# A chunked-attention and MLP kernel on one core: the scores of two heads as a pair of half-row matmuls

## The chip, the core and the metric

The kernel runs on one core of a Trainium2 chip. TensorE multiplies matrices into PSUM, VectorE (DVE), ScalarE (ACT) and GpSimd (POOL) work on SBUF and, but for POOL, on PSUM. DMAs are issued from POOL's queue (loads from DRAM, with a cast from fp32 to fp16) and from SyncE's queue, SP (stores, copies within SBUF, and DMA transposes). The metric is the device time of one execution in microseconds; the kernel before has 217.53 us, the median of five runs from 216.94 to 217.99.

## What is computed

First comes attention in chunks, for 4 batches, 8 heads, 768 tokens and 64 dimensions a head. Each chunk of 32 queries sees 8 memory keys and the keys from 16 tokens before the chunk to 8 tokens after it. Then comes an MLP with a normed input and a residual:

```python
for c in range(S // 32):                      # per batch and head
    k_full = concat([mem_k, k[max(0, 32*c - 16) : min(S, 32*c + 40)]])
    v_full = concat([mem_v, v[the same rows]])
    a = softmax(q_c @ k_full.T / 8)
    out[chunk c] = a @ v_full
x = out as (B, S, 512)                        # heads side by side
xn = (x - mean(x)) / sqrt(var(x) + 1e-6) * g_ln
y = x + relu(xn @ w_ch1) @ w_ch2              # 512 -> 2048 -> 512
```

## The kernel before, in words

**Tiles and units.** The 3072 tokens are 24 tiles of 128, six to a batch. A tile is two groups of 64 queries (two chunks each), so a batch has NG = 12 groups. A group with its neighbours is 88 keys and 8 memory keys, held with gaps in 104 rows (KR). Eight units of three tiles make up the main loop. For each unit TensorE runs 16 up-steps (`up`, L377: one of 16 blocks of the hidden layer for 384 tokens, 4 matmuls) and 12 down-steps (`down`, L394: 4 matmuls of 512 columns). Between the steps a hand-written plan (`at(step, fn, ...)`) puts the attention of the following unit's three tiles, so each engine's order is the order in which the program writes. `attend` takes for each tile the steps of its `scores`, `values`, `norm` and `turn_x`; `root` follows three steps behind `turn_x`.

**Attention of a tile.** `scores` (L289) does 8 matmuls, one for each group and head pair: the stationary operand is a pair's keys, 128 rows (two heads of 64 dimensions), and the moving one is `QZ`, 128 columns: the 64 queries of the first head with zeros in the rows of the second, then the reverse. Then ScalarE does two exps (L296). `values` (L309) does 16 matmuls, each to one half of the output rows, and a column of ones in V gives the sums. `norm` (L319 to L329) is VectorE's. `turn_x` transposes xn, on TensorE with ScalarE's copy (L352, L357) or by a DMA.

**Keys and queries.** For batches 0 and 1 they are loaded in rows of 512 and transposed on TensorE (`turn_kq`, L179); VectorE copies keys to `KT` (`keep_k`, L194), and `keep_q` (L204) copies queries to `QZ`, 64 rows at a time, on ScalarE or VectorE. For batches 2 and 3 `load_tokens` fetches tokens and DMA transposes cross them (`cross_k` to KT, `cross_q` to `QT`, which is `kraw[1]`); POOL spreads QT into QZ (`spread_q`, L277). QZ's other halves are cleared once (`clear_q`, L436). `memv16` holds the memory values with ones; `v_mem` (L136) copies them to V by a DMA on SP.

**PSUM.** There are two `att` slots of two banks, for scores, values and transposes, and four `mm` slots of one bank. An up-step's slot is freed by the relu behind it, on VectorE for even blocks (L385) and ScalarE for odd ones (L383), and is wanted again four steps on.

**The front.** Before the loop a written order handles batch 0's first 6 groups from the first 64 rows of k (48 of q), loaded in two halves of four heads each. POOL's queue is in order k, q (heads 0 to 3), k, q (heads 4 to 7), masks and identity, six V groups, band masks, w1, and the rest. TensorE transposes with `stay_busy` (L366) fillers between, does the g_ln row (L539), the scores of tiles 0 and 1, the values of 0, the scores of 2, the values of 1 and 2, and in between up blocks on tile 0 alone, then on those that have followed. Unit 0 then begins at up-step 8, with `clear_q` for the second buffer at steps 7 and 9.

Of the kernel before, what the change touches and what calls it, by code (L numbers as in the profile page):

```python
# [8 lines left out]
FP32 = mybir.dt.float32  # L9
# [6 lines left out]
def kernel(  # L16
# [29 lines left out]
    memv16 = sb.tile([72, B, H, HD], FP16, name="memv16")[64:72, :, :, :]  # L46
    memv32 = sb.tile([72, 512], FP32, name="memv32")[64:72, :]
# [13 lines left out]
    QT = kraw[1]  # L61
# [4 lines left out]
    QZ = [sb.tile([128, NG, 4, 2, 64], FP16, name=f"QZ{i}") for i in range(2)]  # L66
    AT = [sb.tile([128, 2, H, 64], FP16, name=f"AT{i}") for i in range(3)]
# [73 lines left out]

    def load_w1(c):
        nc.gpsimd.dma_start(
            out=w1c[c], in_=dram(moe_w_ch1, 512 * c, [[FF, 128], [128 * FF, 4], [1, 512]])
        )
# [54 lines left out]
    def keep_q(copy, pv, b, j, par, n, g0, g1):  # L200


        rows = slice(64 * par, 64 * par + 64)
        copy(  # L204
            out=free(QZ[b % 2][rows, g0, j, par, :], 0, [[512, g1 - g0], [8, 8], [1, 8]]),
            in_=free(pv[rows, :], 8 * g0, [[8, g1 - g0], [1, 8], [n, 8]]),
        )

    def kq_block(b, j, g0, g1, kind, last=nc.scalar.copy):

        pk, pq = slot("att"), None
        if kind == "att":
            pq = slot("att")
            pq = [pq[:, i, :] for i in range(2)]
        else:
            pq = [slot("mm")[:, :] for i in range(2)]
        for i in range(2):
            turn_kq(as16(pk[:, i, :]), k16[b % 2], j + i, 96)
        for i in range(2):
            turn_kq(as16(pq[i]), q16[b % 2], j + i, 96)  # L220

        def keep(i):
            keep_k(as16(pk[:, i, :]), b, j + i, 96, g0 + 1 if g0 else 0, g1)
            for par in range(2):
                keep_q(last if i else nc.scalar.copy, as16(pq[i]), b, j + i, par, 96, g0, g1)

        keep(0)
        kept_later.append(lambda: keep(1))
# [11 lines left out]
    def load_tokens(b, which, t):  # L240
        dst, src = ((kraw[0], k), (qraw[0], q))[which]
        nc.gpsimd.dma_start(  # L242
            out=free(dst, 512 * t, [[64, H], [1, 64]]),
            in_=dram(src, b * H * HS + 128 * t * D, [[D, 128], [HS, H], [1, 64]]),
        )

    def cross_k(b, half, t0, t1):
        nc.sync.dma_start_transpose(
            out=free(KT[b % 2], (24 * half + 4 * t0) * KW + 16, [[KW, 4 * (t1 - t0)], [1, 64]]),
            in_=kraw[0][64 * half : 64 * half + 64, 512 * t0 : 512 * t1],  # L250
        )

    def cross_q(half, t0, t1):
        nc.sync.dma_start_transpose(
            out=free(QT, (24 * half + 4 * t0) * 64, [[64, 4 * (t1 - t0)], [1, 64]]),
            in_=qraw[0][64 * half : 64 * half + 64, 512 * t0 : 512 * t1],
        )
# [15 lines left out]
    def spread_q(b, half, t0, t1):  # L273

        for par in range(2):
            rows = slice(64 * par, 64 * par + 64)
            nc.gpsimd.tensor_copy(  # L277
                out=QZ[b % 2][rows, 6 * half + t0 : 6 * half + t1, :, par, :],
                in_=QT[rows, (24 * half + 4 * t0) * 64 : (24 * half + 4 * t1) * 64].rearrange(
                    "p (t j x) -> p t j x", j=4, x=64),  # L280
            )

    def scores(b, t):
        p = slot("att")
        a = AT[t % 3]
        for gg in range(2):
            g = place(b, 2 * t + gg)
            for j in range(4):
                nc.tensor.matmul(  # L289
                    out=p[:, gg, 128 * j : 128 * j + 128],  # L290
                    lhsT=KT[b % 2][:, (4 * g + j) * KW : (4 * g + j) * KW + 128],
                    rhs=QZ[b % 2][:, g, j, :, :],
                    start=True, stop=True,
                )
        for c in range(2):
            nc.scalar.activation(  # L296
                out=free(a, 32 * c, [[512, 2], [64, 8], [1, 32]], KR),
                in_=free(p, 32 * c, [[512, 2], [64, 8], [1, 32]], KR),
                func=ACTF.Exp, bias=band[0:KR, c : c + 1], scale=0.125,
            )  # L300
# [3 lines left out]
    def values(b, t):  # L304
        p = summed[t] = slot("att")
        for h in range(H):
            for gg in range(2):
                c0 = 128 * (h % 4)
                nc.tensor.matmul(  # L309
                    out=p[64 * gg : 64 * gg + 64, h // 4, c0 : c0 + 65],  # L310
                    lhsT=AT[t % 3][0:KR, gg, h, :],
                    rhs=V[b % 2][0:KR, 2 * t + gg, h, 0:65],
                    start=(h % 4 == 0), stop=(h % 4 == 3), tile_position=(0, 64 * gg),
                )
# [119 lines left out]
    def clear_q(i, par):  # L434

        nc.vector.memset(QZ[i][64 - 64 * par : 128 - 64 * par, :, :, par, :], 0.0)  # L436

    def clear_v(i, eng, between=lambda: None):

        eng.memset(V[i][0:32, 0, :, 0:64], 0.0)  # L440
        eng.memset(V[i][64:96, NG - 1, :, 0:64], 0.0)
        eng.memset(V[i][:, :, :, 64:HD], 1.0)
        between()
        for c, g in enumerate((0, NG - 1)):
            eng.tensor_copy(
                out=free(V[i][:, g, 0, 64:65], 0, [[HD, H]]),
                in_=free(counts[:, c : c + 1], 0, [[0, H]]),
            )
# [14 lines left out]
    nc.vector.memset(memv16[:, :, :, 64:HD], 1.0)  # L463
# [3 lines left out]
    for h in (0, 4):  # L467
        for which in range(2):
            load_kq(0, which, 0, CUT[which], h, h + 4)
    keep(counts[:, 0:1], counts[:, 0:1], 16, 0.0)  # L470
    keep(counts[:, 1:2], counts[:, 1:2], -80, 0.0)
    make_identity(nc, identity)
    nc.scalar.copy(out=memk16, in_=memk32)
    nc.scalar.copy(out=memv16[:, 0, :, 0:64], in_=memv32.rearrange("p (h d) -> p h d", h=H))
    stay_busy(10)
    clear_v(0, nc.vector, lambda: clear_q(0, 0))
    clear_q(0, 1)
    clear_k(0)
    mem_keys()
    mem_cols(0)  # L480
    stay_busy(4)
    v_mem(0)
    for g in range(6):
        load_v_group(0, g)
# [10 lines left out]
    nc.gpsimd.tensor_tensor(out=band[:, 1:2], in0=band[:, 1:2], in1=zero3[:, 2:3], op=ALU.add)  # L495
    for c in range(4):
        load_w1(c)
# [21 lines left out]
    for j in range(2):  # L519
        turn_kq(first_k[j], k16[0], j, CUT[0])  # L520
    for j in range(2):
        turn_kq(first_q[j], q16[0], j, CUT[1])
    for j in range(2):
        keep_k(first_k[j], 0, j, CUT[0], 0, 7)
        for par in range(2):
            keep_q(act, first_q[j], 0, j, par, CUT[1], 0, 6)
# [3 lines left out]
    for j in range(2, 4):  # L530
        keep_k(first_k[j], 0, j, CUT[0], 0, 7, act if j == 2 else vec)
# [3 lines left out]
    for g0, g1 in ((0, 2), (2, 6)):  # L535
        for j in range(2, 4):
            for par in range(2):
                keep_q(act if j == 2 else vec, first_q[j], 0, j, par, CUT[1], g0, g1)
    nc.tensor.matmul(out=banks[2], lhsT=ones32, rhs=g_one, start=True, stop=True)  # L539
    nc.vector.tensor_copy(out=g_row, in_=banks[2])  # L540
    scores(0, 0)
    scores(0, 1)
    stay_busy(3)
# [3 lines left out]
    scores(0, 2)  # L547
    values(0, 1)
    norm(1, 1)
    stay_busy(1)  # L550
# [3 lines left out]
    norm(2, 2)  # L554

    for hc in range(3):
        up(0, 1, hc, 0, True)
    turn_x(0, 1, 1)
    up(0, 1, 3, 0, True)
    stay_busy(2)  # L560
    for hc in range(4):
        up(0, 2, hc, 1, True)
    turn_x(0, 2, 2)
    for hc in range(4, 8):
        up(0, 2, hc)
    for hc in range(8):
        up(0, 3, hc, 2)
# [3 lines left out]
    for u, tiles in enumerate(units):  # L571
# [17 lines left out]
        def cross(steps, b, t0, t1, t2):  # L589

            for half in range(2):
                at(steps[half], cross_k, b, half, t0, t1)
                at(steps[2 + half], cross_q, half, t2 - 3, t2)

        def spread(step, b, t0, t1):
            for half in range(2):
                at(step + half, spread_q, b, half, t0, t1)

        if u == 0:
            at(7, clear_q, 1, 0)  # L600
            at(9, clear_q, 1, 1)
            at(10, clear_k, 1)
            at(23, clear_v, 1, nc.gpsimd)
            for j in (0, 2):
                at(15, kq_block, 0, j, 6, NG, "mm", nc.vector.tensor_copy if j else nc.scalar.copy)
                at(15, keep_rest)
# [7 lines left out]
            attend(((17, 19, 19, 22), (18, 21, 21, 24), (20, 23, 23, 26)), "att")  # L614
            at(26, mem_cols, 1)
            at(26, v_mem, 1)
        elif u == 1:
# [8 lines left out]
            attend(((16, 19, 19, 22), (17, 19, 20, 23), (21, 23, 23, 26)), "att")  # L626
        elif following:
            if u in (2, 4):
                attend(((2, 7, 7, 7), (4, 7, 8, 8), (9, 13, 13, 13)))
            else:  # L630
                attend(((9, 14, 14, 14), (11, 14, 15, 15), (16, 20, 20, 20)))
            if u == 2:
# [5 lines left out]
                spread(9, 2, 0, 3)  # L638
                cross((14, 14, 15, 15), 2, 4, 6, 6)
            elif u == 3:  # L640
# [3 lines left out]
                spread(5, 2, 3, 6)  # L644
# [3 lines left out]
            elif u == 4:  # L648
# [7 lines left out]
                spread(23, 3, 0, 3)  # L656
                cross((20, 21, 24, 25), 3, 4, 6, 6)
            elif u == 5:
                at(2, k_around, 3, 4, 6)
                spread(3, 3, 3, 6)  # L660
# [44 lines left out]
```

The softmax here doesn't subtract the row's maximum and nothing guards it: scores larger than these inputs give would overflow.

## Time and profile before

| what | value |
|---|---|
| median of 5 runs | 217.53 us (216.94 to 217.99) |
| the profiled execution's own time | 217.59 us |
| its span on the core | 215.9 us |
| granted TensorE clock | 0.999 |
| scores, L289, TensorE busy | 14.6 us, 192 matmuls |
| values, L309, TensorE busy | 9.5 us, 384 matmuls |
| up, L377 | 89.0 us, 560 matmuls |
| down, L394 | 84.4 us, 368 matmuls |
| exps, L296, ScalarE | 30.3 us, 48 of mean 684 ns |
| spreads of queries, L277, POOL | 13.9 us, 16 of mean 870 ns |
| clears of QZ, L436, VectorE | 5.4 us, 4 of mean 1338 ns |
| memory values by DMA, L136 | 120 KB each |

A profile is one execution. Busy times of TensorE overlap, as a matmul is counted until its result is out while the next has begun, so a matmul's price is read from the chain of work that ended last: its pieces stand in order of time with start and length. A group's line gives the code line, the engine, the operation, out<-in, the count, then busy time and the mean of one, and then the idle time before it with what ended it. PEld is the loading of TensorE's stationary operand, which overlaps PE.

### The profile page before, as it was taken

What the parts mean: (1) busy time and instruction counts of PE and PEld (TensorE: products, weight loads), DVE (VectorE), ACT (ScalarE), POOL (GpSimd) and SP (SyncE); (2) the same over time, 40 slices, a digit from 0 to 9 for tenths busy, and PEclk for the clock granted to TensorE, in tenths of its full rate; (3) what the DMA queues carried; (4) which work ended last, traced back from release to release, by engine and by line L of the source; (5) the groups of instructions that cost most, each with busy time, mean ns of one, the idle gap of its engine ahead of it and who ended that gap; (6) DMA issues with size and microseconds to landing.
All of it is one profiled execution on the core that took longest, in us unless ns stands there. A gap on an engine that the chain in (4) does not pass through costs nothing.

```text
span 215.9 us, 5059 instructions
## 1 busy us (share of the span) xinstructions
PE 209.3 (97%) x2011; PEld 129.6 (60%) x2011; DVE 118.6 (55%) x274; ACT 99.9 (46%) x206; POOL 105.1 (49%) x185
## 2 busy tenths in 40 slices
PE   7899989999999999999999999999999999999992
PEld 2557866557765577446754676457744675466562
DVE  6977774695737639514476359234484437634222
ACT  4478437865893677202753168003761275213100
POOL 7993236799996309974005998425182000300000
PEclk9999999999999999999999999999999999999999
DMA  5999999999999799996313999997643101320012
GB/s 78 180 158 206 209 207 182 199 206 227 150 139 179 89 149 143 151 148 162 45 27 89 144 185 143 149 178 110 162 125 126 49 3 24 98 101 0 0 58 91
DMA packets 87714, 27.37 MB, mean 127 GB/s; under 512 B 78297, under 2 KB 84185, under 8 KB 87642
## 3 DMA queue, kind: packets, MB, share of 16 engines
q0 software_dynamic: 62128, 14.38, 77.3%
q1 hardware_dynamic: 25562, 12.66, 27.7%
q8 instruction: 16, 0.26, 0.5%
q14 instruction: 8, 0.07, 0.1%
HBM read 28.84 MB, written 6.29 MB: 163 GB/s over the span
## 4 chain that ended last, share of the span: by engine, by line
PE 90%; DVE 3%; DMA 3%; ACT 1%; issue 1%; POOL 1%; ACTq 0%; POOLq 0%
PE mm L377 37%; PE mm L394 37%; PE att L289 5%; PE att L309 3%; DMA kraw<-in_k_dram 3%; PE att L179 2%; PE mm L412 2%; DVE QZ L436 1%; PE mm L179 1%; ACT AT L296 1%; PE att L352 1%; DVE rT L385 1%; PE mm L366 1%; PE mm L539 0%; PE att L366 0%
## 5 line engine op out<-in xcount | busy, mean ns | idle before, releaser
L377 PE MATMUL mm<-xT,w1c 128*128 128x384 f16 (+2 forms) x560 | 89.0, 313 | 0.6 <-DVE rT L385 0.5
L394 PE MATMUL mm<-w2c,rT 128*128 128x512 f16 x368 | 84.4, 379 | 0.0
L377 PEld LDWEIGHTS <-w1c 128*128 128x128 f16 x560 | 58.8, 114 | 23.6 <-issue 1.0
L383 ACT ACTIVATE rT<-mm 128x384 f16<-128x384 f32 (+2 forms) x74 | 33.2, 454 | 72.3 <-PE mm L377 50.1
L394 PEld LDWEIGHTS <-rT 128*128 128x128 f16 x368 | 34.7, 98 | 37.5
L385 DVE TENSOR_SCALAR rT<-mm 128x384 f16<-128x384 f32 (+2 forms) x66 | 35.0, 533 | 33.6 <-PE mm L377 33.5
L401 DVE SCALAR_TENSOR_TENSOR osb<-mm,rstd,xs 128x512 f32<-128x512 f32 x23 | 17.3, 751 | 41.8 <-PE mm L394 30.0
L296 ACT ACTIVATE AT<-att,band 104x512 f16<-104x512 f32 x48 | 30.3, 684 | 9.6 <-PE att L289 8.2
L338 POOL TENSOR_SCALAR veps<-squares 128x1 f32<-128x1 f32 x24 | 4.6, 191 | 44.2 <-ACT junk L335 42.9
L117 POOL DMA_DIRECT2D V<-in_v_dram x24 | 18.4, 776 | 10.3 <-DMA w1c<-in_moe_w_ch_dram 7.3
L335 ACT ACTIVATE junk<-xs,nmean 128x512 f16<-128x512 f32 x24 | 17.3, 721 | 7.1 <-DVE nmean L326 6.6
L329 DVE SCALAR_TENSOR_TENSOR xn<-xs,nmean,g_row 128x512 f16<-128x512 f32 x24 | 18.8, 783 | 0.9
L320 DVE SCALAR_TENSOR_TENSOR xs<-att,rec 128x512 f32<-128x512 f32 x24 | 16.6, 691 | 0.8
L277 POOL COPY QZ<-kraw 64x768 f16<-64x768 f16 x16 | 13.9, 870 | 4.0 <-DMA kraw<-qraw 3.4
L289 PEld LDWEIGHTS <-KT 128*128 128x128 f16 x192 | 12.6, 98 | 4.7 <-issue 1.0
L342 POOL TENSOR_TENSOR rstd<-veps,mhalf 128x1 f32<-128x1 f32 x24 | 13.6, 568 | 2.0
L289 PE MATMUL att<-QZ,KT 128*128 128x128 f16 x192 | 14.6, 219 | 0.0
L123 POOL DMA_DIRECT2D V<-in_v_dram x16 | 12.0, 782 | 0.7 <-PE mm L377 0.6
L269 POOL COPY KT<-KT 128x128 f16<-128x128 f16 (+4 forms) x16 | 4.3, 294 | 16.0 <-DMA KT<-kraw 15.9
L309 PEld LDWEIGHTS <-AT 104*64 104x64 f16 x384 | 7.5, 111 | 6.5 <-ACT AT L296 2.1
L242 POOL DMA_DIRECT2D qraw<-in_q_dram x12 | 11.1, 925 | 0.2 <-issue 0.2
L242 POOL DMA_DIRECT2D kraw<-in_k_dram x12 | 11.1, 924 | 0.0
(76 smaller groups left out, 135.4 us busy)
## 6 DMA issues: line engine op xcount, KB each, us to landing
out_dram<-osb SPq DMA_DIRECT2D x23, 256.0 KB, 2.3
V<-in_v_dram POOLq DMA_DIRECT2D x36, 96.0 KB, 6.6
w1c<-in_moe_w_ch_dram POOLq DMA_DIRECT2D x4, 512.0 KB, 9.3
w2c<-in_moe_w_ch_dram POOLq DMA_DIRECT2D x4, 512.0 KB, 13.4
kraw<-in_k_dram POOLq DMA_DIRECT2D x12, 128.0 KB, 4.8
qraw<-in_q_dram POOLq DMA_DIRECT2D x12, 128.0 KB, 5.1
qraw<-in_q_dram POOLq DMA_DIRECT2D x3, 384.0 KB, 11.4
kraw<-in_k_dram POOLq DMA_DIRECT2D x3, 256.0 KB, 6.0
```

The lines of the kernel that those rows point to most:

```text
L117: nc.gpsimd.dma_start(out=V[b % 2][r : r + hi - lo, g, :, 0:64], in_=dram(v, b * H * HS + lo * D, [[64, hi - lo], [HS, H], [1, 64]]),)
L242: nc.gpsimd.dma_start(out=free(dst, 512 * t, [[64, H], [1, 64]]), in_=dram(src, b * H * HS + 128 * t * D, [[D, 128], [HS, H], [1, 64]]),)
L289: nc.tensor.matmul(out=p[:, gg, 128 * j : 128 * j + 128], lhsT=KT[b % 2][:, (4 * g + j) * KW : (4 * g + j) * KW + 128], rhs=QZ[b % 2][:, g ...
L296: nc.scalar.activation(out=free(a, 32 * c, [[512, 2], [64, 8], [1, 32]], KR), in_=free(p, 32 * c, [[512, 2], [64, 8], [1, 32]], KR), func= ...
L320: nc.vector.scalar_tensor_tensor(out=x.rearrange("p (h d) -> p h d", h=H), in0=free(p, 0, [[128, H], [1, 64]]), scalar=1.0, in1=free(r, 0, ...
L329: nc.vector.scalar_tensor_tensor(out=xn[i], in0=x, scalar=nmean[i], in1=g_row, op0=ALU.add, op1=ALU.mult,)
L335: nc.scalar.activation(out=junk, in_=xs[xi], func=ACTF.Square, bias=nmean[i], accum_out=squares[i],)
L377: nc.tensor.matmul(out=p, lhsT=free(w, i, [[4, 128]]), rhs=xT[u % 2][:, dt, lo:hi], start=(dt == 0), stop=(dt == 3),)
L383: nc.scalar.activation(out=o, in_=p, func=ACTF.Relu)
L385: nc.vector.tensor_scalar(out=o, in0=p, scalar1=0.0, scalar2=None, op0=ALU.max)
L394: nc.tensor.matmul(out=p, lhsT=rT[hc][:, 128 * i : 128 * i + 128], rhs=w2c[hc // 4][:, hc % 4, :], start=(hc == 0), stop=(hc == 15),)
L401: nc.vector.scalar_tensor_tensor(out=o, in0=p, scalar=rstd[t % 9], in1=xs[t % 9], op0=ALU.mult, op1=ALU.add,)
```

## The change

`scores` issues two matmuls for each group and head pair, one for each head, on 64 rows each (`tile_position=(64 * par, 0)`) with 64 columns. The two heads go to different banks of the slot, and `AT` and the stationary operand of `values` are indexed accordingly. Queries are kept densely: `QZ` becomes `QT`, two buffers, and `keep_q` copies all 128 rows at once. `spread_q` and `clear_q` are gone, `cross_q` writes QT directly, and batch 3 uses the second raw buffers.

The first memory values come by two VectorE copies (`keep_mem`, groups 0 to 5 in the front and 6 to 11 in unit 0) in place of the DMA. V[0]'s ones are first set in two columns only (two fp16 in one fp32 word), the others at step 13 of unit 0; `memv16`'s ones move to step 14.

In the front the second halves of k and q are issued behind the masks and the identity, three of the six V groups behind the band masks, and four fillers ahead of the first transposes are gone. The scores of tiles 0 and 1 stand in a row as before, but the rest differs: values 0, values 1, scores 2, then the transpose of tile 0, values 2, the transpose of tile 1, each with fillers between; up starts with blocks 0 and 1 on two tiles. In the plan the second tile's scores move to the step of the first.

```diff
-                nc.tensor.matmul(
-                    out=p[:, gg, 128 * j : 128 * j + 128],
-                    lhsT=KT[b % 2][:, (4 * g + j) * KW : (4 * g + j) * KW + 128],
-                    rhs=QZ[b % 2][:, g, j, :, :],
-                    start=True, stop=True,
-                )
+                for par in range(2):
+                    rows = slice(64 * par, 64 * par + 64)
+                    nc.tensor.matmul(
+                        out=p[:, par, 64 * (4 * gg + j) : 64 * (4 * gg + j) + 64],
+                        lhsT=KT[b % 2][rows, (4 * g + j) * KW : (4 * g + j) * KW + 128],
+                        rhs=QT[b % 2][rows, (4 * g + j) * 64 : (4 * g + j) * 64 + 64],
+                        start=True, stop=True, tile_position=(64 * par, 0),
+                    )
...
-                    lhsT=AT[t % 3][0:KR, gg, h, :],
+                    lhsT=AT[t % 3][0:KR, h % 2, 4 * gg + h // 2, :],
...
+    def keep_mem(b, g0, g1, copy):
+
+        src = memv16[:, b, :, 0:64]
+        copy(
+            out=V[b % 2][96:104, g0:g1, :, 0:64],
+            in_=bass.AP(tensor=src.tensor, offset=src.offset,
+                        ap=[list(src.ap[0]), [0, g1 - g0], [HD, H], [1, 64]]),
+        )
...
-    def keep_q(copy, pv, b, j, par, n, g0, g1):
+    def keep_q(copy, pv, b, j, n, g0, g1):
         copy(
-            out=free(QZ[b % 2][rows, g0, j, par, :], 0, [[512, g1 - g0], [8, 8], [1, 8]]),
-            in_=free(pv[rows, :], 8 * g0, [[8, g1 - g0], [1, 8], [n, 8]]),
+            out=free(QT[b % 2], (4 * g0 + j) * 64, [[256, g1 - g0], [8, 8], [1, 8]]),
+            in_=free(pv, 8 * g0, [[8, g1 - g0], [1, 8], [n, 8]]),
         )
...
-    for h in (0, 4):
-        for which in range(2):
-            load_kq(0, which, 0, CUT[which], h, h + 4)
+    for which in range(2):
+        load_kq(0, which, 0, CUT[which], 0, 4)
     keep(counts[:, 0:1], counts[:, 0:1], 16, 0.0)
     keep(counts[:, 1:2], counts[:, 1:2], -80, 0.0)
     make_identity(nc, identity)
+    for which in range(2):
+        load_kq(0, which, 0, CUT[which], 4, H)
...
     scores(0, 0)
     scores(0, 1)
-    stay_busy(3)
+    stay_busy(2)
     values(0, 0)
     norm(0, 0)
     stay_busy(3)
-    scores(0, 2)
     values(0, 1)
     norm(1, 1)
-    stay_busy(1)
+    scores(0, 2)
+    stay_busy(3)
     turn_x(0, 0, 0, "mm")
     stay_busy(3)
     values(0, 2)
     norm(2, 2)
-
-    for hc in range(3):
-        up(0, 1, hc, 0, True)
-    turn_x(0, 1, 1)
-    up(0, 1, 3, 0, True)
     stay_busy(2)
+    turn_x(0, 1, 1, "mm")
+    stay_busy(3)
+
+    for hc in range(2):
+        up(0, 2, hc)
+    turn_x(0, 2, 2, "mm")
+    for hc in range(2, 4):
+        up(0, 2, hc)
     for hc in range(4):
-        up(0, 2, hc, 1, True)
-    turn_x(0, 2, 2)
+        up(0, 3, hc, 2)
     for hc in range(4, 8):
-        up(0, 2, hc)
-    for hc in range(8):
-        up(0, 3, hc, 2)
+        up(0, 3, hc)
...
         if u == 0:
-            at(7, clear_q, 1, 0)
-            at(9, clear_q, 1, 1)
-            at(10, clear_k, 1)
+            at(9, clear_k, 1)
+            at(11, keep_mem, 0, 6, NG, vec)
+            at(13, nc.vector.memset, V[0].bitcast(FP32)[:, :, :, 33 : HD // 2], TWO_ONES)
+            at(14, nc.vector.memset, memv16[:, :, :, 64:HD], 1.0)
...
-            attend(((17, 19, 19, 22), (18, 21, 21, 24), (20, 23, 23, 26)), "att")
+            attend(((17, 19, 19, 22), (17, 21, 21, 24), (20, 23, 23, 26)), "att")
...
-            attend(((16, 19, 19, 22), (17, 19, 20, 23), (21, 23, 23, 26)), "att")
+            attend(((16, 19, 19, 22), (16, 19, 20, 23), (21, 23, 23, 26)), "att")
...
-                attend(((2, 7, 7, 7), (4, 7, 8, 8), (9, 13, 13, 13)))
+                attend(((2, 7, 7, 7), (2, 7, 8, 8), (9, 13, 13, 13)))
             else:
-                attend(((9, 14, 14, 14), (11, 14, 15, 15), (16, 20, 20, 20)))
+                attend(((9, 14, 14, 14), (9, 14, 15, 15), (16, 20, 20, 20)))
```

## The prediction

> **What bounds the kernel now.** I read the page first (busy shares, then the chain that ended last), then the pieces of that chain in order of time, then the groups by line, and at last the timeline of two places, the first 31 us and one up-stage. The page says that TensorE is nearly always busy and that the chain is TensorE's own:
>
> ```profile
> PE 209.3 (97%) x2011; PEld 129.6 (60%) x2011; DVE 118.6 (55%) x274; ACT 99.9 (46%) x206; POOL 105.1 (49%) x185
> ...
> PE 90%; DVE 3%; DMA 3%; ACT 1%; issue 1%; POOL 1%; ACTq 0%; POOLq 0%
> ```
>
> So work taken from TensorE counts in full, and work taken from POOL or VectorE counts only where TensorE stands. The chain in order of time prices TensorE's pieces; here is part of the last unit that scores tiles:
>
> ```profile
> 174.41 0.45 PE att L289 x8
> 174.86 1.30 PE mm L377 x8
> ...
> 178.55 0.63 PE att L309 x32
> 179.18 0.77 PE mm L377 x4
> ...
> 184.72 0.37 PE att L309 x16
> 185.09 6.15 PE mm L394 x28
> ```
>
> Columns: start, length, piece. The scores of a tile (L289) cost 0.45 us, 56 ns for each of 8 matmuls, and the piece behind them is undisturbed: 8 matmuls of 384 columns in 1.30, the same 162.5 ns each as elsewhere. The values (L309) work on halves of the array: 16 in 0.37, 32 in 0.63, so 0.26 for 16 more, 16.3 ns each, and 0.11 for getting in. The piece behind pays too: 0.77 where 4 x 162.5 = 0.65, 6.15 where 28 x 215.7 = 6.04. Getting out costs about 0.11.
>
> The front follows a load, then TensorE's hand-written order:
>
> ```profile
> 2.75 6.01 DMA kraw<-in_k_dram
> ...
> 8.80 0.69 PE mm L179 x32
> 9.49 0.97 PE att L366 x4
> 10.46 0.61 PE mm L179 x32
> 11.08 1.05 PE mm L539 x2
> 12.13 0.57 PE att L289 x8
> ...
> 21.01 3.32 PE mm L377 x44
> ...
> 25.03 1.34 DVE QZ L436
> ...
> 27.22 1.34 DVE QZ L436
> ...
> 29.02 1.46 PE mm L377 x8
> ```
>
> The second half of k's heads lands at 8.76; transposes, fillers and the g_ln matmul run without a gap to the first scores. Later two clears of QZ hold VectorE's evictions back: TensorE stands 0.55 us before 29.02 (timeline).
>
> **Part 1, scores on half rows.** 192 matmuls of 128 columns become 384 of 64 columns on 64 rows, two at a time. The trace has no half-row matmul, so I bound it. Floor: two run wholly together, 64 columns at the 162.5/384 = 0.42 ns a column of L377 plus 2.5 ns = 29 ns a pair, 0.23 us a tile, plus 0.22 in and out. The nearest row is L309, half-column, 65 columns: 32.6 ns a pair, 0.26 plus 0.22. I take 0.25: a tile alone costs 0.47 (+0.02 against 0.45), two in a row 0.72 (-0.18 against 0.90). The upper end depends on the weight load:
>
> ```profile
> L289 PEld LDWEIGHTS <-KT 128*128 128x128 f16 x192 | 12.6, 98 | 4.7 <-issue 1.0
> L309 PEld LDWEIGHTS <-AT 104*64 104x64 f16 x384 | 7.5, 111 | 6.5 <-ACT AT L296 2.1
> ```
>
> A contiguous load of 128 columns (98 ns) is shorter than one of 64 columns into a half-column tile (111): a quick path exists and the half-column tile misses it. If half-row loads miss it too, 128 columns stream like L309's 64 at double length: 0.42 x 128 = 53 ns plus L309's surplus of 5 over its own 27, about 58 ns a pair, 0.47 a tile, 0.69 alone (+0.24), 1.16 for two (+0.26). The Trainium skill ("TensorEngine Tiling (Array Packing)", Restrictions and Gotchas) lists the quick load as lost under column tiling and doesn't list row tiling; no run here shows which, and I take the kept path.
>
> A rule speaks against the change: the same page (Instruction Overhead) says a matmul of one column is no quicker than one of 60, with the advice not to tile a dimension that is already small, and "TensorE: Matmul & The Clock Gate" (Part 1) puts the floor between starts at 25 ns. By it 16 starts are 0.40, a tile alone 0.62 (+0.17), two 1.02 (+0.12), and seven units 7 x 0.29 = 2.0 us more. But L309's 65-column matmuls start every 16.3 ns on two tiles. The row decides.
>
> In each of the seven units that attend a following one, two tiles are scored in a row and one alone: -0.18 + 0.02 = -0.16, in all **-1.12 us**, all on TensorE's path.
>
> **Part 2, what the second scores wait for and whom they hold up.** Both score slots are free: the values that used them were normed in the unit before; in unit 0 the key copies leave them by about 34.5, scores start at 35.15. But four exps now stand in a row on ScalarE. In units 2 and 4 (step 2) relu of hc 3 is queued behind them and its buffer is wanted by step 7:
>
> ```profile
> 76.95 1.26 ACT L296 ACTIVATE AT<-att,band 104x512 f16<-104x512 f32 x2 [0.61 <-PE att L289]
> ...
> 78.11 0.49 ACT L383 ACTIVATE rT<-mm 128x384 f16<-128x384 f32 x1
> ```
>
> Two exps take 1.16 (76.95 to 78.11). Scores start at 76.31 on TensorE; exps then run from 76.87 to 79.19, relu to 79.68. TensorE reaches step 7 at 76.31 + 0.72 + 4 x 0.65 = 79.63. Stall 0.1 with the semaphore, twice: **+0.2** (between 0 and 0.3 each, if exps drag to 1.27 a pair). In units 3, 5 and 6 (step 9) the next ScalarE relu is hc 11, wanted by step 15, five steps on: no stall. In units 0 and 1 the steps are down-steps, evicted by VectorE; values come two or more steps of 0.86 later, past 2.4 us of exps for the first tile. Zero.
>
> **Part 3, queries dense.** POOL's 16 spreads (13.9 us) vanish; TensorE never waited for them, zero. Query copies use all 128 rows, half as many instructions (ScalarE 790 ns each for 768 columns): they lie under the transposes and downs, zero. The transposes write QT by themselves on SP, no DMA is added there, and both QT buffers are long free. The v_mem load of 120 KB becomes two VectorE copies of 3072 elements on 8 partitions. Nearest is L169 (COPY, f16, SBUF to SBUF, 384 elements, mean 307 ns; 8 elements take 181 at L445): 0.33 ns an element, 1.2 us. The other end is PSUM speed (L194, 1065 ns for 880): 3.3 us. I take 1.2.
>
> **Part 4, the front.** POOL now does counts and identity (0.85 us) between the two halves of k and q, and three V loads move behind the band masks. The queue still holds 459 KB of k and q when the second half is issued at 3.6 to 4.8, at about 190 GB/s, so landing stays at 8.76 (bounds: 0.2 earlier, since the 120 KB v_mem transfer is gone; 0.85 later). V groups 4, 5 landed by 15.5 behind a full queue and are wanted at 17.57; w1 is issued at 10.8 as before. VectorE's clears of QZ and most of V's ones (1.34 each) go; VectorE waited for k anyway. keep_mem runs about 8.0 to 9.2, before k's second half is turned: hidden; at 3.3 us it would delay the last copies to 12.8 and cost 0.7. Scores start at 12.06 as now.
>
> From there, by trace durations: first exps 0.08 earlier, values(0) at 14.02 (14.10); its norm ends at 16.49, the next at 18.31, the third at 20.14, as VectorE takes 1.9 each and does them back to back. TensorE: values(1) 15.20, scores(2) 15.57, turn_x(0) 16.70, values(2) 17.57, turn_x(1) 18.48. ScalarE's copy of it ends 19.46, so up on two tiles starts at 19.52: 8 x 0.109 = 0.87, turn_x(2) 0.22, 0.87 more, to 21.48; xT of tile 2 is copied by 21.59; 16 matmuls of 128 columns at 56 ns end at 22.48, 16 of 384 at 25.08. Before, tile 0 alone was multiplied in time now filled with fillers, and hc 7 ended at 21.01 + 16 x 0.109 + 32 x 0.056 = 24.53. **+0.55.**
>
> Then steps 8 to 15, 32 x 162.5 ns = 5.2: before 24.53 to 30.32 with the stall, after 25.08 to 30.28 without. VectorE there does 4 relus (2.2), clear_k 0.65, keep_mem 1.2, V's rest by the memset rows (85 ns for 32, 218 for 192) 0.6, memv16 0.5: 5.15 in 5.2, no block longer than the two buffers' slack. **-0.59.** If keep_mem took 3.3, a stall of about 0.5 comes back.
>
> **Sum:** -1.12 + 0.2 + 0.55 - 0.59 = -0.96. The profiled execution took 217.59 (span 215.9 and 1.7 around it), which gives 216.63; it lies 0.06 over the median of 217.53, so I say **216.6**.
>
> **Rivals.** (a) *Half-row loads miss the quick path.* One mechanism, TensorE's weight load in the scores: 7 x (0.26 + 0.24) = 3.5, front and stalls +0.1, 221.1. It turns slower once a pair takes over (1.35 - 0.44)/24 = 38 ns. For it: double columns on half an array are unseen here. Against: the PEld rows tie the loss to half columns. (b) *The front gives it back*: k lands 0.85 late, or keep_mem is slow: 216.6 + 0.8 = 217.4. For it: the whole front hangs on one landing. Against: the queue is full. (c) *More gain*: getting in and out by rows is cheap and pairs take 29 ns, so 0.5 for two and 0.25 alone: 7 x -0.6 = -4.2 at most; half of that is 214.5. Against: both crossings show 0.11 wherever the array is split.
>
> **Numbers.** Main 0.63, (a) 0.17, (b) 0.14, (c) 0.06. Main alone spans 215.9 to 217.3 (0.04 of a tile's 0.25 either way, stalls 0 to 0.6, front 0.4). The range 215.2 to 218.4 takes in (b) and the near side of (c), and leaves out (a). This kernel's measurement tells 0.3% (0.65 us) from no change: faster means under 216.88. Main gives 0.52 there, 0.09 within and 0.02 slower; (c) 0.06 faster; (b) 0.10 within and 0.04 slower; (a) 0.17 slower. Faster 0.58, same 0.19, slower 0.23.
>
> **What would show it.** L289 with 16 in about 0.36 and 32 in 0.61, and 0.11 on the piece behind; two L289 pieces less per unit; in units 2 and 4 a wait of L377 for ScalarE's relu of 0.1; no QZ; the second k landing near 8.8; hc 7 ending near 25.1 and the first L179 behind it at 30.3. Pairs over 38 ns, or scores beginning past 12.5, make it wrong.

## The result, and the profile after

The changed kernel takes 217.48 us, the median of 44 executions, beside 217.71 for the kernel before (79); compared execution by execution the ratio is 0.9973, 95% interval 0.996 to 0.9986, so 0.6 us less. A second set of 22 executions on another occasion gave 0.9951 (0.9933 to 0.9969), 1.1 us less. The forecast of 0.96 us less lies between. These ratios leave out executions over 1.5% above a kernel's fastest, four of the 44, and three of those four had the fallen clock that this section is about; with all 44 the means are 217.48 and 217.84, 0.4 us apart, and the counts and medians below leave out none.

What is unlike before is the spread: at full clock 215.04 to 218.1, and one at 221.2, where the kernel before has 216.88 to 218.86. The profiled execution (217.94 us, span 216.2) is one of the long ones and shows why. First its chain that ended last, start, length and piece:

```profile
12.15 0.36 PE att L287 x16
...
14.56 1.39 PE mm L364 x3
...
31.44 0.80 PE att L187 x32
...
76.91 0.57 PE att L287 x32
77.48 3.48 PE mm L375 x20
...
101.38 8.36 DMA V<-V
...
109.87 0.70 PE att L307 x32
...
175.52 0.57 PE att L287 x32
176.09 3.37 PE mm L375 x20
...
181.73 0.34 PE att L287 x16
182.07 3.56 PE mm L392 x16
```

The scores do what was forecast, and a little more. A tile alone is 0.34 and leaves 0.11 on the piece behind it (3.56, where 16 x 215.7 ns are 3.45): 0.45, as before. Two in a row are 0.57 and leave 0.12 (3.37, where 20 x 162.5 ns are 3.25): 0.69 where they were 0.90. The 16 further matmuls cost 0.23, 14.4 ns each or 28.8 a pair: two half-row matmuls run together, as 29 ns was the prediction's floor for a pair. (The floor's 2.5 ns a matmul comes out of the chain: 215.7 ns for 512 columns and 162.5 for 384 are 0.416 a column and nearly 3 besides.) In unit 2 the piece behind is 3.48, so the relu's 0.1 is there too.

Two lines don't belong to the scores. The three fillers at 14.56 take 1.39 us, where three of 216 ns take 0.65. And L307 at 109.87 comes behind a DMA, V<-V. The profile's answer by stages, with the granted clock in the third column from the end, tells of the first; here the changed kernel's profiled execution:

```profile
12.00:14.00 2.00, 1.35 (x39) 0.73 (x40) 0.69 (x1) 1.41 (x3) 2.00 (x4) 0.96 1.64 106
14.00:17.00 3.00, 3.00 (x51) 1.67 (x51) 2.13 (x7) 1.01 (x2) 2.79 (x5) 0.50 1.05 159
```

and the same stages of the same kernel in another execution (x1_again, 215.4 us):

```profile
12.00:14.00 2.00, 1.35 (x45) 0.76 (x36) 0.51 (x1) 1.77 (x4) 2.00 (x4) 1.00 1.69 111
14.00:17.00 3.00, 3.00 (x45) 1.43 (x45) 2.73 (x9) 2.10 (x5) 2.75 (x5) 1.00 1.14 171
```

The kernel before has there:

```profile
12.00:14.00 2.00, 1.79 (x20) 1.11 (x19) 1.32 (x3) 1.39 (x4) 2.00 (x4) 1.00 2.52 144
```

TensorE was as idle from 12 to 14 us in both executions of the changed kernel (1.35 busy of 2.00, before 1.79), yet in one its clock then fell to a half and in the other not. In stretches of 0.1 us the half clock lasts from 13.83 to 17.25, so 3.4 us; the two other profiles with a fall, x5_half_pairs and x11_before_fill below, have 11.91 to 15.32 and 12.36 to 15.77, also 3.4. That agrees with the window of some 3.4 us over which, by the Trainium skill ("TensorE: Matmul & The Clock Gate", Part 1), activity is judged on a clock that runs free of the kernel. Over 216 us, a granted clock of 0.992 is 3.5 us at half clock and 0.984 is 6.9, one and two such windows. The clock of every execution is on record, but for the 79 of the kernel before beside the first set, so the falls can be counted without a profile.

| kernels | executions | clock under 0.995 | median at full clock | median under |
|---|---|---|---|---|
| before | 94 | 8 | 217.59 | 218.56 |
| changed (both sets) | 66 | 29 | 216.70 | 217.72 at 0.989 to 0.992, 218.30 at 0.984 |
| changed, five fillers for two (five variants) | 44 | 1 | 216.12 | 217.94 |
| before, no fillers there | 22 | 6 | 217.17 | 218.8, as the three at 0.983 |
| before, five fillers for three | 12 | 3 | 217.61 | 218.95 |
| before, half-row scores (x4) | 20 | 1 | 217.11 | 217.72 |
| before, half-row scores in pairs (x5) | 6 | 2 | 215.92 | 216.84 |
| the same, five fillers for three (x8) | 6 | 1 | 216.19 | 217.07 |

At full clock the change is worth 217.59 - 216.70 = 0.89 us. In 29 of 66 executions 1.0 to 1.6 us come back. The sets come from several occasions: the changed kernel has 23 falls of 44 in the first set and 6 of 22 in the second, beside which the kernel before had 2 of 27 and the variants with five fillers none of 11.

### The profile page after: what moved, and what is told of

The parts are those of the page before. It is cut to its first block, busy times and chain, and to the rows that moved or that the text cites. A ratio compares the mean times of both kernels' runs of the same rounds, so it can differ in the third digit from the quotient of the medians.

```text
span 216.2 us, 5336 instructions
## 1 busy us (share of the span) xinstructions
PE 209.9 (97%) x2173; PEld 124.8 (58%) x2173; DVE 113.4 (52%) x268; ACT 91.1 (42%) x187; POOL 92.2 (43%) x169
## 4 chain that ended last, share of the span: by engine, by line
PE 90%; DMA 4%; DVE 3%; SPq 1%; ACT 1%; issue 0%; DVEq 0%; ACTq 0%
PE mm L392 38%; PE mm L375 33%; PE mm L364 4%; DMA V<-V 4%; PE att L307 4%; PE att L287 3%; PE att L187 2%; PE mm L187 2%; PE mm L410 2%; PE att L364 1%; DVE xn L327 1%; DVE xs L318 1%; PE att L350 1%; ACT AT L294 1%; PE mm L533 0%
## 5 line engine op out<-in xcount | busy, mean ns | idle before, releaser
L375 PE MATMUL mm<-xT,w1c 128*128 128x384 f16 (+2 forms) x528 | 87.9, 322 | 0.2 <-DVE rT L383 0.2
L375 PEld LDWEIGHTS <-w1c 128*128 128x128 f16 x528 | 57.9, 114 | 24.8 <-issue 0.6
L381 ACT ACTIVATE rT<-mm 128x384 f16<-128x384 f32 (+2 forms) x66 | 31.7, 484 | 76.3 <-PE mm L375 54.9
L383 DVE TENSOR_SCALAR rT<-mm 128x384 f16<-128x384 f32 (+2 forms) x66 | 35.6, 542 | 33.7 <-PE mm L375 33.3
L294 ACT ACTIVATE AT<-att,band 104x512 f16<-104x512 f32 x48 | 29.5, 688 | 12.1 <-PE att L287 10.4
L336 POOL TENSOR_SCALAR veps<-squares 128x1 f32<-128x1 f32 x24 | 5.6, 231 | 53.1 <-ACT junk L333 51.8
L327 DVE SCALAR_TENSOR_TENSOR xn<-xs,nmean,g_row 128x512 f16<-128x512 f32 x24 | 18.0, 752 | 0.9
L307 PEld LDWEIGHTS <-AT 104*64 104x64 f16 x384 | 7.9, 114 | 8.6 <-issue 4.4
L307 PE MATMUL att<-V,AT 104*64 104x65 f16 x384 | 9.9, 201 | 1.7 <-DMA V<-V 1.0
L364 PE MATMUL mm<-busy 128*128 128x512 f16 x26 | 9.7, 510 | 1.2 <-DVE counts L456 1.2
L317 DVE RECIPROCAL rec<-att 128x8 f32<-128x8 f32 x24 | 4.9, 203 | 11.3 <-PE att L307 7.1
```

What stands on the lines that cost most here:

```text
L294: nc.scalar.activation(out=free(a, 32 * c, [[512, 2], [64, 8], [1, 32]], KR), in_=free(p, 32 * c, [[512, 2], [64, 8], [1, 32]], KR), func= ...
L307: nc.tensor.matmul(out=p[64 * gg : 64 * gg + 64, h // 4, c0 : c0 + 65], lhsT=AT[t % 3][0:KR, h % 2, 4 * gg + h // 2, :], rhs=V[b % 2][0:KR ...
L327: nc.vector.scalar_tensor_tensor(out=xn[i], in0=x, scalar=nmean[i], in1=g_row, op0=ALU.add, op1=ALU.mult,)
L364: nc.tensor.matmul(out=p, lhsT=busy[:, 0:128], rhs=busy, start=True, stop=True)
L375: nc.tensor.matmul(out=p, lhsT=free(w, i, [[4, 128]]), rhs=xT[u % 2][:, dt, lo:hi], start=(dt == 0), stop=(dt == 3),)
L381: nc.scalar.activation(out=o, in_=p, func=ACTF.Relu)
```

## The experiments

Each is named by its label; the ratio is to the kernel before, beside which it ran.

**The changed kernel again.** No edit.

> The changed kernel, unchanged, for a second profile. Theory (two losses outside the scores): the scores gain their 1.5 us, and two things take it back, a fall of TensorE's clock to half in the front between about 14 and 17 us in some executions, and a wait of about 1 us of the values in unit 3 for the copy V<-V. Then executions with a granted clock near 0.984 lie 1.0 to 1.5 us above those near 1.0, and a profile at full clock has its first 96-row transposes near 30.3 (not 31.4) and still the V<-V wait at about 109. Rival A (the front's new order is longer by itself): those transposes stay near 31 at full clock. Rival B (the V<-V wait was one execution's accident): no such wait here.

0.9951 (0.9933 to 0.9969); 6 of 22 executions under 0.995, their medians 218.0 at 0.984 and 216.5 at full clock. The profile is at full clock, and its chain answers rival A:

```profile
11.78 0.36 PE att L287 x16
...
13.99 0.75 PE mm L364 x3
...
29.81 0.80 PE att L187 x32
...
76.03 3.47 PE mm L375 x20
...
104.00 3.37 PE mm L375 x20
107.37 0.63 PE att L307 x31
```

The fillers take 0.75, and the 96-row transposes stand at 29.81, earlier than 30.48 in the old kernel: the new order isn't longer. Counted from the scores' start it is 18.03 us, and 18.0 to 18.1 in the three variants with five fillers that didn't wait for w1 there, where the old order took 18.35. No V<-V wait is here, so that part of the theory, a wait in each execution, is wrong; it comes in some.

**Five fillers.**

```diff
     scores(0, 1)
-    stay_busy(2)
+    stay_busy(5)
```

> The changed kernel with five fillers in place of two behind the first two tiles' scores; they end at about 13.7, before the values can start at 13.9, so they cost no time. Theory: the clock no longer falls, all executions are near 1.0, and the median falls by 0.4 to 0.8 us against the changed kernel, to about 0.994 of the kernel before. Rival A: clock or not, the order is what costs; the median moves by less than 0.2 us.

> The changed kernel with five fillers once more, beside the two that follow, on the same chip. Theory: no execution under 0.995 of the clock, and a median of 0.990 to 0.994 of the kernel before.

The first gave 0.9906 (0.9892 to 0.992) with 5 executions, all at 1.0; its median of 215.76 is 1.0 us under that of x1_again, more than the clock was to give. The second gave 0.9954 (0.9927 to 0.998) with 12, one of them at 0.992. So nearly all of the clock's falls go (with the four variants below, 1 in 44 against 29 in 66), but the gain in the median isn't settled by these two: the second falls outside its expectation on both counts. Something else scatters the executions at full clock, 215.4 to 217.8. The first's profile names one thing, in the timeline:

```profile
12.11 1.25 PE L364 MATMUL mm<-busy 128*128 128x512 f16 x5
...
19.81 0.41 PE L375 MATMUL mm<-xT,w1c 128*128 128x256 f16 x2 [1.04 <-DMA w1c<-in_moe_w_ch_dram]
```

The five fillers end before the values; then the first up stands 1.04 us for w1's first quarter. The second's profile has a V<-V wait of 0.9 and one of 0.5 for w2.

**V<-V sooner**, with five fillers.

```diff
                 cross((14, 14, 15, 15), 2, 4, 6, 6)
+                at(24, v_mem, 2)
+                at(24, v_around, 2)
             elif u == 3:
-                at(1, v_mem, 2)
-                at(1, v_around, 2)
```

> The five fillers, and batch 2's memory values and the copy V<-V issued at step 24 of unit 2 in place of step 1 of unit 3, some 5 us sooner. Theory: the values of unit 3 wait no more and another 0.7 to 1.0 us falls off wherever the wait was: about 0.990 of the kernel before. Rival B: equal to the run with fillers alone.

0.9931 (0.9904 to 0.9958). Unit 3 waits for nothing, but unit 5 waits 0.7 us for batch 3's own V<-V, issued where it always was: no verdict from the time. Over all profiles with the copy at its old step, three of six of the changed kind wait 0.8 to 1.0 us in unit 3, none of six of the old kind, though their values come as soon after the issue (7.3 to 7.6 us, against 7.4 to 7.5). The copy lands within 7.4 us in some executions and after 8.1 to 8.4 in others. Whether the change makes the late landing likelier, or three of six is luck, stays open.

**Half rows and pairs in the kernel before**, its front, QZ and spreads kept. The diff of the scores is the change's own, with this moving operand; the first of the two kernels leaves the plan as it was, the second moves the pairs too.

```diff
-                        rhs=QZ[b % 2][:, g, j, :, :],
+                        rhs=QZ[b % 2][rows, g, j, par, :],
```

> The kernel before with only the scores on half rows; the plan, the front, QZ and the spreads stay. Theory: a tile alone costs 0.45 us as before (0.11 in, 0.23, 0.11 out), so the units gain nothing; the first two tiles' scores stand in a row and gain 0.2, and the shorter scores may let the clock fall: within 0.3% of the kernel before, with some executions under 0.992. If the crossings in and out were nothing: 24 x 0.22 = 5 us faster. If the half-row weight load were slow: 5 us slower.

> The kernel before, its front, spread queries and clears kept, with only the scores on half rows (the moving operand is the half of QZ that is not zero) and the second tile's scores at the first one's step. Theory: seven pairs at 0.21 us less each, plus 0.2 in the front, less 0.1 each in units 2 and 4 where a relu stands behind four exps: 1.4 us less, 0.9935, if the V<-V wait does not bite; 0.5 us less if it does. Rival A, which blames the front: the full 1.4. If the scores themselves did not pay: no change.

Half rows alone: 0.9974 (0.9962 to 0.9987), just within the 0.3% expected; of the executions under 0.992 that were expected there is none, and one of 20 at 0.992. In the chain each tile is 0.34 and leaves 0.11 or 0.12:

```profile
174.28 0.34 PE att L291 x16
174.62 1.42 PE mm L379 x8
176.04 0.34 PE att L291 x16
176.38 2.08 PE mm L379 x12
```

(8 x 162.5 ns = 1.30, 12 are 1.95.) From the first 96-row transposes to the last unit's start it takes 160.89 us, the kernel before 160.76: no gain in the units; its front is 0.23 shorter (30.25 for 30.48), what the one pair there should give. The rest of the 0.6 us is not accounted for. With pairs: 0.9925 (0.9906 to 0.9944), 1.6 us less, and the 1.1 between the two fits the crossings saved (7 x 0.22, less 0.2 for the relus, is 1.3). Two of its six executions are under 0.995, the profiled one among them:

```profile
12.11 1.03 PE att L291 x32
...
12.00:14.00 2.00, 2.00 (x36) 1.20 (x35) 1.33 (x3) 1.38 (x4) 1.98 (x4) 0.50 2.93 140
```

The clock is at half before the scores begin at 12.11, and they run at half speed themselves, 1.03 us for 0.57. Up to there TensorE's order is that of the kernel before, and in the 3.4 us ahead of the fall it was busy for 3.2. So here the shorter scores didn't make the clock fall. With half rows alone, whose front is the same, it is 3 falls in 26 executions, not clearly more than the 8 in 94 of the kernel before.

**Pairs with more fillers**: the last kernel, `stay_busy(5)` for `stay_busy(3)` behind the first two tiles' scores.

> Half-row scores in pairs in the kernel before, with five fillers in place of three behind the first two tiles' scores. Theory: no clock under 0.995, and 0.4 to 0.6 us less than the same without the added fillers, about 0.990 of the kernel before. Against the changed kernel with five fillers (0.9906) this compares the two fronts and the dense queries: my step by step count has them 0.04 us apart, so equal within 0.3 us. Rival A (the new front is longer): this one is faster by 0.5 us or more.

0.9938 (0.9914 to 0.9962), where 0.990 was expected; one execution in six is at 0.992. The fillers gained nothing to be seen, against expectation. It isn't faster than the changed kernel with fillers, which speaks against rival A once more.

**Fewer fillers in the kernel before**, and more, as a control: `stay_busy(3)` behind the first two tiles' scores taken out, and made five.

> The kernel before with the three fillers behind the first two tiles' scores taken out and nothing else. TensorE then stands 1.0 us more before the values at 14.1, which wait for the exps anyway. Theory (the clock falls when TensorE does too little between about 10.5 and 13.9): full-size scores or not, some executions now show a granted clock of 0.984 to 0.992 and are 1.0 to 1.5 us longer, and the spread over executions grows to that of the changed kernel; the median rises by 0.3 to 1.3 us. Rival (the clock falls for something else in the changed kernel, such as half-row matmuls): no execution under 0.992, no change of the median.

> Control: the kernel before with five fillers in place of three behind the first two tiles' scores. Theory: its clock fell in few executions anyway, so the median stays within 0.15%, and executions under 0.995 vanish. If fillers sped the kernel up by themselves, apart from the clock, this would fall by 0.5 us too.

Without them: 1.0001 (0.9983 to 1.0019), so the median did not rise as expected. But six of 22 executions fell under 0.995, three of them at 0.983 with 218.8 to 219.2 us, far over the 217.17 of the others; none of the 94 of the kernel before is under 0.99. The fall needs no half-row matmul. That less work on TensorE before 14 us makes it likelier fits, but 6 of 22 beside 5 of 41 on the same occasion doesn't settle it, and the profiled execution had no fall. With five: 1.0016 (0.9991 to 1.0042), three of 12 under 0.995, where none was expected: the fillers don't speed the kernel by themselves, nor did they keep the clock here. Its stages and its timeline show why:

```profile
12.00:13.00 1.00, 1.00 (x9) 0.74 (x9) 0.96 (x3) 0.37 (x1) 1.00 (x2) 0.68 4.31 86
...
12.26 1.83 PE L289 MATMUL att<-QZ,KT 128*128 128x128 f16 x16
13.89 2.18 PE L366 MATMUL mm<-busy 128*128 128x512 f16 x5
16.00 0.44 PE L309 MATMUL att<-V,AT 104*64 104x65 f16 x16
```

The clock fell at 12.36, as the scores began, so the fillers came too late, and at half clock five of them last 2.18 us and push the values out to 16.00. Fillers can't keep a clock that falls ahead of them. TensorE was busy for nearly all of the 3.4 us ahead of this fall, so idle time alone doesn't explain it. What lies in the stretch ahead of all three profiled falls is the g_ln row (L539 here, 1.05 us of matmuls on one row); no run moves it, so whether it counts as little work stays open.

**Pairs one step later**: five fillers, and

```diff
-                attend(((2, 7, 7, 7), (2, 7, 8, 8), (9, 13, 13, 13)))
+                attend(((3, 7, 7, 7), (3, 7, 8, 8), (9, 13, 13, 13)))
```

> The changed kernel with five fillers, and in units 2 and 4 both scores of the pair at step 3 in place of step 2, so that relu of hc 3 is ahead of the four exps and the next one behind them is wanted five steps on. Theory: the 20 matmuls behind the pair take 3.37 us in place of 3.47 in both units, 0.2 us in all, which the median of a few executions hardly tells. If the values at step 7 come to wait for the later exps: no gain, and the wait stands at L307.

0.9934 (0.9912 to 0.9956). The chain shows the stall gone (2.72 for 16 is 2.60 and the crossing), and behind it a V<-V landing late again:

```profile
73.50 2.60 PE mm L375 x16
76.10 0.57 PE att L287 x32
76.68 2.72 PE mm L375 x16
...
99.87 8.14 DMA V<-V
```

**Band masks ahead of the V loads**, with five fillers.

```diff
-    for g in range(3):
-        load_v_group(0, g)
...
-    for g in range(3, 6):
+    for g in range(6):
         load_v_group(0, g)
```

> The five fillers, and POOL's band masks ahead of all six V loads instead of between the third and the fourth. POOL's instructions are the same, only their order differs. In the changed kernel the DMAs move 61 to 93 GB/s between 10 and 11 us, where the kernel before moves 176, because the masks hold back the last V loads; so w1's first quarter lands at 18.6 to 19.8, and the first up wants it at about 19. Theory: the dip is filled, w1's first quarter lands at least 0.5 us sooner, no wait of L375 for w1 is left, and the median falls by 0.1 to 0.6 us against fillers alone. Rival (the landing of w1 is set by how fast the queue moves, not by the dip): it lands as late as before, no gain.

0.9924 (0.9894 to 0.9954), inside the spread of fillers alone. The dip is still there (90 GB/s from 10 to 11 us), w1's first quarter landed 7.9 us after its issue at 11.51, so at 19.4, and the waits keep the line

```profile
PE mm L375 <- DMA w1c<-in_moe_w_ch_dram: 0.7, 1, 0.7
```

My reason for the late w1 fell; in the next kernel, with the same order, it landed at 17.65. What moves it between 17.65 and 19.8 stays open.

**All together.** The edits of this section's variants of the changed kernel at once.

> All that promised something together: five fillers, band masks ahead of the V loads, batch 2's copy V<-V at step 24 of unit 2, pairs of scores at step 3 in units 2 and 4. Theory: 0.2 us from the relus on top of the run with fillers and masks, and no wait for V<-V in unit 3: 0.988 to 0.990 of the kernel before, and a narrower spread than any other changed version.

0.9923 (0.9892 to 0.9953), a median of 215.81 us of nine, from 214.95 to 217.15. That is 1.7 us under the kernel before, and the lowest execution of all is its; but it isn't 0.988 to 0.990, nor narrow, nor told apart from fillers alone or from the changed kernel's 0.9951, whose interval overlaps.

## Why the prediction came out as it did

- **Part 1, the scores.** Mechanism right, size a little small: two tiles in a row take 0.69 (0.72 forecast), one alone 0.45 (0.47), a unit saves 0.21 (0.16). A pair of matmuls takes 28.8 ns, the floor; L309, the nearest row, takes 32.6 and has the longer weight loads, though no run shows that they are why. The half-row load keeps the quick path, which disposes of rival (a). The answer for the line:

```profile
L287 PEld LDWEIGHTS <-KT x384: 92/95/129, 12.1 to 181.8; 64*128 64x128 f16 x192
```

  Median 95 ns: even below the full load's 98, far from the half-column load's 112. The floor of 25 ns between starts that the prediction cites (the Trainium skill, "TensorE: Matmul & The Clock Gate", Part 1) does not bind two row tiles: 14.4 here.
- **Part 2, the relus.** Right: 0.1 in unit 2 and in unit 4 each, none in units 3, 5 and 6, and gone when the pair moves a step. Not foreseen was a second wait in unit 2, 0.1 to 0.2 us for a relu that VectorE does behind two norms (0.16 at 86.60 in the profiled execution); in the kernel before TensorE doesn't stand there.
- **The units together.** From the start of unit 0's transposes to the last unit's start, 160.76 before and 189.58 - 29.81 = 159.77 in x1_again: -0.99; forecast -1.12 + 0.2 = -0.92. Two errors nearly cancel here: the pairs gain 7 x 0.21 = 1.47, and besides the 0.2 of part 2 the second wait in unit 2 and longer transposes in unit 0 of this execution (0.86 us for 0.68) take some of it back. Four other profiles with pairs and no late copy have -1.07 to -1.18.
- **Part 4, the front.** In x1_again -0.67 (29.81 for 30.48), forecast -0.04. The old end was misread by 0.16: the piece at 29.02 lasts 1.46, so to 30.48, and I had reckoned 30.32. Of the -0.67, 0.35 is an earlier start of the scores (11.78 for 12.13): k's second half lands at 8.46, not 8.76, and I had granted 0.2 for that. In the profiled execution after it landed sooner still, at 8.16, but TensorE's first 32 transposes took 1.06 us there, 0.69 in x1_again, and the scores began at 12.15. The remaining 0.3 is the new order, 18.03 us from scores to transposes where I counted 18.2 and the old one took 18.35. This front is one of the best: the six profiles with five fillers have the transposes at 29.71 to 30.68. `keep_mem` took 0.96 us (1.2 forecast) and hid; the clears' stall of 0.55 went. "w1 is issued at 10.8 as before" was wrong: 11.46, as masks and three V loads precede it, and the loads' slack became a wait in some executions.
- **The term that was missing.** I reckoned the front at full clock and priced the removed fillers at nothing. Shorter scores, two fillers in place of three there and four fewer earlier leave TensorE less to do before 14 us, and the clock falls in 29 of 66 executions, 8 of 94 before. In the profiled execution TensorE was busy for 2.86 of the 3.43 us ahead of the fall, in x2_fill, with five fillers, for all of the same stretch. 12 executions at +1.6 us and 11 at +1.0 in the first set of 44 are 0.7 us on the average. The kernel before loses 0.1 by its own falls, so 0.89 at full clock becomes 0.3; all 44 give 0.4, and the ratio's 0.6 leaves out three of the twelve. It is no rival of mine: (b) named k's landing and `keep_mem`.
- **Luck.** That 0.89 at full clock is so near to 0.96 is in part luck. The terms of x1_again add up to -0.67 - 0.99 = -1.66, and its 215.40 lies 1.1 us under its own set's median at full clock: what the front and the pairs gain over the forecast, other executions give back in waits for loads. (Another 0.5 us between the two profiles compared lies behind the last unit, where the old one stands 3.78 us after its last `osb` and all thirteen others, old kernel's variants too, 3.1 to 3.3; that is no effect of the change.) In rival (c), half of 4.2 us off 217.53, with the other terms' +0.16, is 215.6, not 214.5.

Shown: the pairs' gain, the price of a crossing, the quick load, the price of a fall, and that with five fillers nearly all of the changed kernel's falls are gone. Only argued: that TensorE's idle time is what lets the clock fall, as the two falls in the old front don't fit it; which of the removed fillers and the shorter scores count; and that the scatter at full clock (quartiles 216.07 and 217.21, before 217.30 and 217.86) comes from DMA landings; waits for V<-V, w1 and w2 of 0.5 to 1.0 us stand in several profiles, but no variant removed the scatter.

## What to carry to other kernels

Splitting the array pays by the visit, not by the matmul: each visit cost some 0.22 us in and out here, so put split work in a row before you make it shorter. Work that looks like padding on the busiest engine may be holding its clock; when you shorten real work near it, count busy time in that stretch afresh, as a hint and no more, and look at the granted clock of many executions, not of one profile. When the bound engine gets ahead by a microsecond, every load that was just in time is a wait to come: list the landings with less slack than the gain.

## What the runs showed of the hardware that was not expected

- TensorE's clock at half for 3.4 us at a time (13.83 to 17.25 in the profile after), in the same program on some executions and not on others, at 1.0 us for a granted clock of 0.992 and 1.6 for 0.984; in two of three profiled cases it fell after a stretch in which TensorE was busy for over 90% of the time.
- Two half-row matmuls of 64 columns together every 28.8 ns, each with its own 128-column weight load.
- The same copy V<-V, issued at the same step, landing within 7.4 us or after 8.1 to 8.4.
